# A decode step of two attention and two MLP layers: each 8 MB cache load split into even and odd partitions on two DMA queues

## The chip, the cores and the metric

The kernel runs on one core of one Trainium2 chip. The core's engines are TensorE (PE, with its weight loads as PEld), VectorE (DVE), ScalarE (ACT), GpSimd (POOL) and SyncE (SP, which here only issues DMAs); 16 DMA engines move the data between the chip's main memory (HBM) and the on-chip memory. The metric is the device time of one execution in microseconds (us), as the median of several runs; lower is better.

## What is computed

Two layers of attention over a cache, each followed by a gated MLP, for a batch of 2 and one new token each. Cut to what matters here:

```python
B, Sq, D = 2, 1, 576
H, Sk, Dh = 32, 8192, 128            # k_cache and v_cache: (B, H, Sk, Dh) float32, 268 MB each

def attention(x):
    q = (x @ wq) split into H heads of Dh
    scores = einsum("bhqd,bhkd->bhqk", q, k_cache) * Dh ** -0.5
    o = einsum("bhqk,bhkd->bhqd", softmax(scores), v_cache)
    return o joined @ wo

def mlp(x):
    return (gelu(x @ w_gate) * (x @ w_up)) @ w_down      # 576 -> 4608 -> 576

x = x + attention(layernorm(x));  x = x + mlp(layernorm(x))
x = x + attention(layernorm(x));  x = x + mlp(layernorm(x))
```

Both attention layers read the whole of both caches, so nearly every byte is read twice.

## The kernel before, in words

One work item of attention is a pair of heads of one batch entry (30 pairs), or one head alone (the last two heads, 4 items; the kernel calls them singles). Layer 0 takes the 30 pairs and then the singles, layer 1 the same in reverse order, so that some cache data of the singles can stay on the chip between the layers.

**Memory.** One tile, `space`, holds everything that is loaded: 128 partitions by 24 parts and a little more; a part is 2048 float32 per partition. For the pairs it is three slots of 8 parts, at parts 0, 8 and 16 (`slots0` and `slots1`, lines 255 and 256). The keys of a pair fill one slot and its values another, so that K and V of pair after pair go round the three slots. A slot's load is 128 partitions by 16384 float32, 8192 KB; partition p gets one contiguous piece of 64 KB.

**Order of the loads.** All loads stand in one queue in the program, `sp.queue`, in a fixed order. `pump` (line 97) issues the load at its head as soon as the program has reached the point at which its place is free; `done` (line 157) frees a place and pumps. For the pairs that makes two points for each item n: when the last products of K(n) have been summed (`add_up`, line 652), its slot takes V(n+1), and when `values(n)` (line 731) has used V(n), its slot takes K(n+2). Each load is one DMA on SyncE's queue (line 171). The tile framework, not the kernel, adds the semaphore waits: each instruction waits for those whose data it reads or overwrites, as far as the framework can tell their regions of `space` apart.

**The work of one item.** `multiply(n, unit)` (line 617) takes the keys in five units of 2, 2, 2, 1 and 1 parts. VectorE multiplies the keys by the query in place (line 637: input and output are the same region of `space`), GpSimd adds the two halves of each row in place (line 642), VectorE sums the rest to scores (line 656). Then come the maximum (line 691 and 698 on VectorE, with TensorE between and after), the exponentials on ScalarE (line 705 and 709), and `values(n)`: 64 matrix products on TensorE that read the slot of V(n) (line 739). What they made is gathered later, during item n+1 (lines 755 to 774). VectorE runs its instructions in order, so the first multiplication of item n+1 stands right behind the maximum of item n.

In the first 6 items of layer 1 and the last 4 of layer 0 a quarter of the rows of a unit is summed by ScalarE (line 646) in place of GpSimd. Weights (`rows`, `middle`, `out_rows`, `down` and so on) are loaded by DMAs of their own on SyncE's queue, at line 185 and the like. In layer 1 the first pair's K and V come in halves of 4 parts each. So 8-part loads are K and V of 30 pairs in layer 0 without the first K, which comes in two halves, and of 29 pairs in layer 1: 59 and 58, 117 in all.

The functions that the diff touches, and what calls them:

Of the kernel before, what the change touches and what calls it, by code (L numbers as in the profile page):

```python
# [24 lines left out]
PART = 16 * DH  # L25
# [106 lines left out]
def decode_layers(ctx, tc, x_in, kc, vc, wq, wo, wg, wu, wd, out):  # L132
    nc = tc.nc
# [8 lines left out]
    space = consts.tile([P, END], F32, name="space")  # L142
# [19 lines left out]
    def cache(kind, layer, item, at, lo=0, hi=None, skip=0):  # L162

        hi = item.parts if hi is None else hi
        src = {"k": kc, "v": vc}[kind][item.b, item.h:item.h + item.heads].rearrange("h s d -> (h s) d")
        src = src.rearrange("(p j) d -> p (j d)", p=P)
        base = (kind, layer) + item.name

        def load(a):
            at_of[base] = a - skip - lo * PART  # L170
            nc.sync.dma_start(space[:, a:a + (hi - lo) * PART - skip], src[:, lo * PART + skip:hi * PART])

        sp.queue.append(([base + (k,) for k in range(lo, hi)], at + lo * PART + skip, (hi - lo) * PART - skip, load))

# [842 lines left out]
```

## Time and profile before

| | before |
|---|---|
| median of 3 runs | 2685.91 us (2685.9 to 2685.99) |
| the profiled execution, its own time | 2685.71 us |
| its span, first to last instruction | 2683.9 us |
| VectorE busy | 1863.1 us (69%) |
| GpSimd busy | 1143.9 us (43%) |
| TensorE busy | 935.0 us (35%) |
| ScalarE busy | 180.5 us (7%) |
| read from HBM | 1151.6 MB |

The span is what the trace covers; 1.8 us of the execution's own time lie outside it. Busy times are sums over an engine's instructions. A row of the timeline has the start in us from the span's start, the duration, the engine, the line, the operation and its tiles; in brackets stands the idle time before it on its engine and what ended it. "SPq" and "ACTq" are the sequencers of SyncE and ScalarE issuing a DMA; that row's start is when the issue's waits were over.

### The profile page before, as it was taken

To read this page: it belongs to the slowest core of one execution; us is meant where nothing else is said; L and a number is where in the kernel's file an instruction comes from. 1 tells how busy PE (TensorE), PEld (TensorE's weight loads), DVE (VectorE), ACT (ScalarE), POOL (GpSimd) and SP (SyncE) were. 2 spreads that over 40 slices of the span, in tenths; PEclk is the share of its full clock that TensorE was granted. 3 is DMA by queue.
4 is the path that set the end of the run, shared out by engine and by line. 5 is a ranking of instruction groups with operands and counts; after the bars stand their busy time and mean duration, and the time that the engine had idled before them with its cause. 6 is when DMAs were issued, how large, how long until landed. Compare 5 with 4: busy or idle time off the path is not lost.

```text
span 2683.9 us, 18550 instructions
## 1 busy us (share of the span) xinstructions
PE 935.0 (35%) x7356; PEld 328.4 (12%) x7356; DVE 1863.1 (69%) x1349; ACT 180.5 (7%) x918; POOL 1143.9 (43%) x342
## 2 busy tenths in 40 slices
PE   2322332233233323326665233233323332332255
PEld 0010111011001101102221011001100110110022
DVE  5578777867777787787158777787677778777750
ACT  0000000000000000003013100000000000000000
POOL 2345444544544454454024444454454445444530
PEclk7656665665666566657986666566656656665667
DMA  9999999999999999999999999999999999999998
GB/s 422 435 437 426 432 436 436 432 429 434 434 433 432 433 433 434 434 427 420 408 410 436 435 433 433 433 430 432 437 434 431 430 435 436 434 426 436 435 422 375
DMA packets 37911, 1152.81 MB, mean 430 GB/s; under 512 B 4272, under 2 KB 4928, under 8 KB 16448
## 3 DMA queue, kind: packets, MB, share of 16 engines
q1 hardware_dynamic: 37800, 1151.62, 99.8%
q8 instruction: 58, 0.95, 0.1%
q14 instruction: 29, 0.24, 0.0%
q10 hardware_dynamic: 24, 0.01, 0.0%
HBM read 1151.60 MB, written 0.00 MB: 429 GB/s over the span
## 4 chain that ended last, share of the span: by engine, by line
DMA 27%; DVE 13%; PE 7%; POOL 6%; issue 1%; ACT 1%; POOLq 0%; SPq 0%; ACTq 0%; DVEq 0%
DMA space<-in_A_k_cache_dram 19%; DVE space L637 8%; POOL space L642 6%; PE acc L739 6%; DVE S L656 4%; DMA space<-in_B_w_down_dram 3%; DMA space<-in_B_w_gate_dram 1%; DMA space<-in_A_v_cache_dram 1%; DMA space<-in_B_w_up_dram 1%; DMA space<-in_A_wq_dram 1%; DVE osb L757 1%; ACT prz L709 1%; DMA space<-in_A_wo_dram 1%; PE xps L784 0%; PE sm L700 0%
## 5 line engine op out<-in xcount | busy, mean ns | idle before, releaser
L642 POOL TENSOR_TENSOR space<-space 128x2048 f32<-128x2048 f32 (+3 forms) x332 | 1140.4, 3443 | 1315.5 <-DVE space L637 1211.1
L637 DVE TENSOR_TENSOR space<-space,qp 128x4096 f32<-128x4096 f32 (+2 forms) x329 | 1126.9, 3441 | 460.9 <-DMA space<-in_A_k_cache_dram 450.5
L656 DVE TENSOR_REDUCE S<-space 128x32 f32<-128x2048 f32 (+3 forms) x332 | 581.9, 1753 | 114.9 <-POOL space L642 112.0
L739 PE MATMUL acc<-space,prz 128*8 128x512 f32 x4096 | 594.4, 743 | 8.1 <-issue 6.7
L768 PE MATMUL spare<-weights,osb 128*64 128x2 f32 (+1 forms) x528 | 70.8, 256 | 1199.6 <-ACT osb L759 1183.1
L768 PEld LDWEIGHTS spare<-weights,osb 128*64 128x64 f32 (+1 forms) x528 | 65.2, 208 | 1216.2 <-ACT osb L759 1198.1
L739 PEld LDWEIGHTS acc<-space,prz 128*8 128x8 f32 x4096 | 112.8, 103 | 423.3 <-issue 418.7
L693 PE MATMUL sm<-ident,m 128*1 128x128 f32 x68 | 24.9, 366 | 330.1 <-DVE m L691 330.1
L759 ACT COPY osb<-osb 128x128 f32<-128x128 f32 x60 | 17.9, 298 | 1731.5 <-DVE osb L757 1731.5
L757 DVE SCALAR_TENSOR_TENSOR osb<-acc,diag,osb 128x128 f32<-128x128 f32 x204 | 71.5, 351 | 7.2
L462 POOL TENSOR_TENSOR rstd<-ve,mhalf 128x2 f32<-128x2 f32 x4 | 2.8, 700 | 162.7 <-DVE ve L461 162.7
L719 PE MATMUL sm<-rs,one 128*128 128x2 f32 x120 | 34.9, 360 | 81.1 <-ACT prz L709 81.1
L646 ACT ACTIVATE space<-space 128x128 f32<-128x128 f32 x188 | 55.6, 297 | 66.5 <-DVE space L637 51.1
L709 ACT ACTIVATE prz<-S,nbs 64x128 f32<-64x128 f32 (+1 forms) x136 | 53.4, 393 | 3.1
L693 PEld LDWEIGHTS sm<-ident,m 128*1 128x1 f32 x68 | 5.4, 79 | 342.1 <-DVE m L691 309.4
L700 PE MATMUL sm<-m,one 1*128 1x2 f32 (+1 forms) x136 | 38.7, 351 | 22.8 <-DVE m L698 22.7
L698 DVE TENSOR_REDUCE m<-sm 1x2 f32<-1x128 f32 (+1 forms) x68 | 18.9, 278 | 32.5 <-PE sm L693 32.5
L719 PEld LDWEIGHTS sm<-rs,one 128*128 128x128 f32 x120 | 29.7, 307 | 86.3 <-ACT prz L709 86.3
L755 DVE TENSOR_SCALAR osb<-acc,diag 128x128 f32<-128x128 f32 x68 | 23.3, 342 | 23.7 <-PE acc L739 23.7
L903 DVE STREAM_TRANSPOSE turned<-acc 128x288 f32<-128x288 f32 x4 | 1.9, 483 | 52.2 <-PE acc L892 52.2
L705 ACT ACTIVATE nbs<-sm 128x2 f32<-128x2 f32 (+1 forms) x68 | 11.7, 172 | 390.7 <-PE sm L700 390.7
L700 PEld LDWEIGHTS sm<-m,one 1*128 1x128 f32 x136 | 32.8, 298 | 41.3 <-DVE m L698 41.1
(130 smaller groups left out, 452.3 us busy)
## 6 DMA issues: line engine op xcount, KB each, us to landing
space<-in_A_k_cache_dram SPq DMA_DIRECT2D x8, 4096.0 KB, 19.1
space<-in_A_v_cache_dram SPq DMA_DIRECT2D x3, 4096.0 KB, 21.1
space<-in_A_v_cache_dram SPq DMA_DIRECT2D x6, 2048.0 KB, 32.8
space<-in_B_w_gate_dram SPq DMA_DIRECT2D x18, 576.0 KB, 8.2
space<-in_B_w_up_dram SPq DMA_DIRECT2D x18, 576.0 KB, 7.8
space<-in_A_wo_dram SPq DMA_DIRECT2D x16, 576.0 KB, 8.7
space<-in_A_wo_dram SPq DMA_DIRECT2D x8, 1152.0 KB, 27.3
space<-in_B_w_gate_dram SPq DMA_DIRECT2D x2, 4608.0 KB, 19.6
```

Of the source, the lines that this page charges most:

```text
L637: nc.vector.tensor_tensor(out=u, in0=t, in1=qp_of(n)[:, 0:DH].unsqueeze(1).to_broadcast([P, r1 - r0, DH]), op=ALU.mult)
L642: nc.gpsimd.tensor_tensor(out=half, in0=half, in1=u[:, :r2 - r0, DH // 2:], op=ALU.add)
L646: nc.scalar.activation(row, row, AF.Copy, accum_out=S[n][:, 16 * lo + r:16 * lo + r + 1])
L656: nc.vector.tensor_reduce(out=S[n][:, r0:r1], in_=half, axis=AX.X, op=ALU.add)
L693: nc.tensor.transpose(peaks[n], m, ident)
L700: nc.tensor.matmul(low[n], one[0:1, :].to_broadcast([1, P]), m1, start=True, stop=True)
L709: nc.scalar.activation(prz[rows_, 0:item.rows // 4, e, :], s[rows_, 0:item.rows].rearrange("p (g r) -> p g r", r=4), AF.Exp, bias=nbs[rows ...
L719: nc.tensor.matmul(tot, ones, rs[:, n % 2, :], start=True, stop=True)
L739: nc.tensor.matmul(acc_of(n)[32 * c:32 * c + 8, :], prz[:, g, :, :].rearrange("p e r -> p (e r)"), space[:, at:at + 4 * DH], start=(g < 4) ...
L755: nc.vector.tensor_scalar_mul(t, q[:, 0, :], diag[:, 0:1])
L757: nc.vector.scalar_tensor_tensor(t, q[:, r, :], diag[:, r:r + 1], t, op0=ALU.mult, op1=ALU.add)
L768: nc.tensor.matmul(to[:, i, 0:item.heads], t[:, i:item.heads * DH:GH], w, start=True, stop=True,)
```

## The change

A load of eight parts becomes two DMAs. The even partitions (`space[0::2, ...]`, 64 partitions by 16384) go to SyncE's queue and the odd ones (`space[1::2, ...]`) to ScalarE's. Loads of fewer parts stay one DMA on SyncE's queue. Five lines are added, so the lines below 171 count 5 more in the changed kernel: 637 becomes 642, 691 becomes 696, and so on.

```diff
         def load(a):
             at_of[base] = a - skip - lo * PART
-            nc.sync.dma_start(space[:, a:a + (hi - lo) * PART - skip], src[:, lo * PART + skip:hi * PART])
+            queues = (nc.sync, nc.scalar) if hi - lo == 8 else (nc.sync,)
+            step = len(queues)
+            for r, queue in enumerate(queues):
+                queue.dma_start(
+                    space[r::step, a:a + (hi - lo) * PART - skip], src[r::step, lo * PART + skip:hi * PART]
+                )
```

The instructions of the built programs, engine by engine, show where the new DMAs stand and what waits for them. Names in brackets are semaphores that an instruction waits for. DVE, PE, Activation and Pool count an engine's finished instructions; DMAHW0 to DMAHW7 count landed DMAs, and the DMAs take the eight in turn.

**SyncE**, from the load of V(1) on, before: one DMA for each load, alternately V (after a DVE count) and K (after a PE count).

```order
L171 DMA space<-in_A_v_cache_dram 128x16384 [waits DMAHW4_49,DMAHW1_49,DVE_49]
L171 DMA space<-in_A_k_cache_dram 128x16384 [waits DMAHW2_49,PE_49]
L171 DMA space<-in_A_v_cache_dram 128x16384 [waits DMAHW3_49,DVE_49]
L171 DMA space<-in_A_k_cache_dram 128x16384 [waits DMAHW4_49,PE_49]
L171 DMA space<-in_A_v_cache_dram 128x16384 [waits DMAHW5_49,DVE_49]
```

The same place of SyncE now: the same sequence of loads with 64 partitions each.

```order
L174 DMA space<-in_A_v_cache_dram 64x16384 [waits DMAHW1_49,DVE_49]
L174 DMA space<-in_A_k_cache_dram 64x16384 [waits DMAHW3_49,PE_49]
L174 DMA space<-in_A_v_cache_dram 64x16384 [waits DMAHW5_49,DVE_49]
L174 DMA space<-in_A_k_cache_dram 64x16384 [waits DMAHW7_49,PE_49]
L174 DMA space<-in_A_v_cache_dram 64x16384 [waits DMAHW1_49,DVE_49]
```

The other 64 partitions are with **ScalarE**. Its instructions of item 0 and the start of item 1's, before (nbs and prz are the softmax, osb and oT the gathering):

```order
L705 ACTIVATE nbs<-sm_125 128x2 [waits PE_49]
L709 ACTIVATE prz,rs<-S,nbs 64x32x4 [waits Activation_49]
L709 ACTIVATE prz,rs<-S,nbs 64x32x4
L759 COPY osb<-osb 128x128 [waits DVE_49]
L774 COPY oT<-spare 32x4 [waits PE_49]
L774 COPY oT<-spare 32x4
L705 ACTIVATE nbs<-sm_126 128x2 [waits PE_49,Activation_49]
```

And now, from the load of V(1) on:

```order
L174 DMA space<-in_A_v_cache_dram 64x16384 [waits DMAHW1_49,DVE_49]
L710 ACTIVATE nbs<-sm_125 128x2 [waits PE_49]
L714 ACTIVATE prz,rs<-S,nbs 64x32x4 [waits Activation_49]
L714 ACTIVATE prz,rs<-S,nbs 64x32x4
L174 DMA space<-in_A_k_cache_dram 64x16384 [waits DMAHW2_49,PE_49]
L764 COPY osb<-osb 128x128 [waits DVE_49]
L779 COPY oT<-spare 32x4 [waits PE_49]
L779 COPY oT<-spare 32x4
L174 DMA space<-in_A_v_cache_dram 64x16384 [waits DMAHW4_49,DVE_49]
L710 ACTIVATE nbs<-sm_126 128x2 [waits PE_49,Activation_49]
```

Two DMA issues, each with its wait, have come into every item of ScalarE: the V load stands ahead of the softmax, the K load between the softmax and the gathering.

**VectorE** before, from the end of item 1 to the start of item 2: the first multiplication waits for one DMA, which is K(2).

```order
L691 TENSOR_REDUCE m<-S 128x1 [waits DVE_49]
L698 TENSOR_REDUCE m_302<-sm_126 1x2 [waits PE_49]
L637 TENSOR_TENSOR space<-space,qp_123 128x4096 [waits DMAHW5_49]
L637 TENSOR_TENSOR space<-space,qp_123 128x4096
L656 TENSOR_REDUCE S<-space 128x32 [waits Activation_49,Pool_49]
```

The same place now:

```order
L696 TENSOR_REDUCE m<-S 128x1 [waits DVE_49]
L703 TENSOR_REDUCE m_307<-sm_126 1x2 [waits PE_49]
L642 TENSOR_TENSOR space<-space,qp_123 128x4096 [waits DMAHW4_49,DMAHW5_49,DMAHW3_49,DMAHW2_49]
L642 TENSOR_TENSOR space<-space,qp_123 128x4096
L661 TENSOR_REDUCE S<-space 128x32 [waits Activation_49,Pool_49]
```

The counts that belong to these four waits name the two halves of V(2) (on 2 and 3) and the two halves of K(3) (on 4 and 5). The halves of K(2), on 0 and 1, are no longer waited for here: item 1's first multiplication has waited for them, together with those of V(1) on 6 and 7. So it goes on through the pairs of both layers: the first multiplication of item n waits for V(n) and K(n+1), which are loaded into the other two slots. The matrix products of `values(n)` wait for the two halves of V(n) alone, as they waited for the one DMA before.

## The prediction

> **What bounds the kernel now.** I read the page's slices first: is any resource busy from end to end?
>
> ```profile
> PE 935.0 (35%) x7356; PEld 328.4 (12%) x7356; DVE 1863.1 (69%) x1349; ACT 180.5 (7%) x918; POOL 1143.9 (43%) x342
> DMA  9999999999999999999999999999999999999998
> q1 hardware_dynamic: 37800, 1151.62, 99.8%
> ```
>
> The DMA engines are, in all 40 slices, and everything comes from one queue, q1, SyncE's. Next, the rate by stretches (the last two columns are DMA share and GB/s): the pairs of layer 0, and the first MLP with its small pieces.
>
> ```profile
> 60.00:560.00 500.00, 156.48 (x1045) 51.63 (x1045) 359.51 (x224) 22.25 (x101) 226.89 (x63) 0.61 1.00 433
> 1262.00:1402.00 140.00, 91.42 (x1262) 38.27 (x1258) 40.12 (x91) 11.47 (x66) 12.37 (x9) 0.90 1.02 406
> ```
>
> A load of 8192 KB (8.389 MB) at 433 GB/s takes 19.37 us, and K and V of a pair 38.75. The timeline of one item shows how the engines stand to that.
>
> ```profile
> 502.16 0.33 SPq L171 DMA_DIRECT2D space<-in_A_v_cache_dram  x1
> 503.93 0.17 ACT L705 ACTIVATE nbs<-sm 128x2 f32<-128x2 f32 x1 [5.90 <-PE sm L700]
> 510.62 8.75 DVE L637 TENSOR_TENSOR space<-space,qp 128x4096 f32<-128x4096 f32 x2 [7.43 <-DMA space<-in_A_k_cache_dram]
> 514.34 0.33 SPq L171 DMA_DIRECT2D space<-in_A_k_cache_dram  x1
> 540.86 0.33 SPq L171 DMA_DIRECT2D space<-in_A_v_cache_dram  x1
> 544.39 9.70 PE L739 MATMUL acc<-space,prz 128*8 128x512 f32 x64
> 549.33 8.75 DVE L637 TENSOR_TENSOR space<-space,qp 128x4096 f32<-128x4096 f32 x2 [7.44 <-DMA space<-in_A_k_cache_dram]
> 554.16 0.33 SPq L171 DMA_DIRECT2D space<-in_A_k_cache_dram  x1
> ```
>
> Item n's multiplication starts at 510.62, when K(n) has landed, and the next at 549.33: 38.71 us, the DMA time of two loads. The compute of K(n) takes until 540.86, 30.24 us, when its slot is given to V(n+1); K(n+2) follows at 554.16, when the matrix products have used V(n). So VectorE waits 7.4 us for each K, and the DMAs never stop, **because two loads are still queued or running while K(n) is being worked on**. That is what the change touches.
>
> **The change part by part.** *The added waits.* The rows of VectorE in the section on the change show that the first multiplication of item n now waits for V(n) and K(n+1). Put this on the timeline above: the multiplication that starts at 510.62 would have to wait for a K load that is issued only at 514.34. The wait cannot be met early; it binds in every item. While it lasts all three slots are full (K(n), V(n), K(n+1)), so no load can be issued until K(n) is worked off. The multiplication and the loads, which overlapped, go one after the other:
>
> - at 0 the multiplication starts, and the DMAs are idle;
> - at 30.24 K(n)'s slot is free and V(n+1) is issued into an empty queue;
> - at about 43.5 (554.16 less 510.62) `values(n)` is done and K(n+2) is issued, behind the running V(n+1), without a gap;
> - V(n+1) and K(n+2) land, and item n+1 starts.
>
> What a load into an empty queue costs beside its bytes is shown by the first load of the program. It has 4096 KB, and SyncE's fourth DMA (line 207) waits for it to land:
>
> ```profile
> 0.73 0.39 SPq L171 DMA_DIRECT2D space<-in_A_k_cache_dram  x1
> 12.87 0.54 SPq L207 DMA_DIRECT2D space<-in_A_wq_dram  x1
> SPq L207 <- DMA space<-in_A_k_cache_dram: 9.6, 1, 9.6
> ```
>
> 4.194 MB at 433 GB/s are 9.69 us; from issue to the waiter's start it is 12.14, so start and landing cost 2.45. The period is 30.24 + 2.45 + 38.75 = **71.44 us** in place of 38.71. The last pair of a layer waits for its V alone: 30.24 + 2.45 + 19.37 = 52.06.
>
> How many periods there are, from the multiplications' starts: second and last pair of layer 0, first, second and last pair of layer 1.
>
> ```profile
> 84.61 8.75 DVE L637 TENSOR_TENSOR space<-space,qp 128x4096 f32<-128x4096 f32 x2 [17.86 <-DMA space<-in_A_k_cache_dram]
> 1171.45 8.75 DVE L637 TENSOR_TENSOR space<-space,qp 128x4096 f32<-128x4096 f32 x2 [7.53 <-DMA space<-in_A_k_cache_dram]
> 1439.41 4.40 DVE L637 TENSOR_TENSOR space<-space,qp 128x4096 f32<-128x4096 f32 x1
> 1475.39 8.75 DVE L637 TENSOR_TENSOR space<-space,qp 128x4096 f32<-128x4096 f32 x2 [6.37 <-DMA space<-in_A_k_cache_dram]
> 2562.91 8.75 DVE L637 TENSOR_TENSOR space<-space,qp 128x4096 f32<-128x4096 f32 x2 [7.48 <-DMA space<-in_A_k_cache_dram]
> ```
>
> Layer 0: pair 0, which started long before 84.61, now waits for V(0) and K(1), and K(1)'s landing is what 84.61 waited for. So pair 0 starts at 84.61, and the last one 28 periods and one short one later: 84.61 + 28 x 71.44 + 52.06 = 2137.0, against 1171.45: **+965.5**. Layer 1: pair 0 now waits for K(1), whose landing 1475.39 waited for; the last pair starts 2052.4 later, against 2562.91 - 1475.39 = 1087.5: **+964.9**. Three items near the layers' starts have a compute of 27 to 28.5 us in place of 30.24, which these rows bound (pair 0 of layer 1 is worked off when V(1) is issued):
>
> ```profile
> 37.13 8.75 DVE L637 TENSOR_TENSOR space<-space,qp 128x4096 f32<-128x4096 f32 x2 [9.89 <-PE qp L595]
> 65.62 0.33 SPq L171 DMA_DIRECT2D space<-in_A_v_cache_dram  x1
> 1467.96 0.33 SPq L171 DMA_DIRECT2D space<-in_A_v_cache_dram  x1
> 1502.54 0.33 SPq L171 DMA_DIRECT2D space<-in_A_v_cache_dram  x1
> ```
>
> That is 28.49, 28.55 and 27.15, together 6.5 less than three times 30.24. Behind each layer's last pair the work goes on as before, except that V of that pair has landed where it was just being loaded; this lead is worth between nothing and one load, 19.37 us, per layer. The next loads wait for slots that the last pair's compute frees at an unchanged distance, which speaks for nothing; I take 0 and keep 39 for the range.
>
> Sum: 965.5 + 964.9 - 6.5 = 1923.9 us on the profiled execution's 2685.7 (its span of 2683.9 and 1.8 outside; the median is 0.2 more): **4610 us**.
>
> *The second issue, on ScalarE.* 117 issues; the longest that I found of this line takes 0.59 us.
>
> ```profile
> 13.45 0.59 SPq L171 DMA_DIRECT2D space<-in_A_k_cache_dram  x1
> ACT osb L759 <- DVE osb L757: 1731.5, 60, 40.1
> ```
>
> The V issue stands ahead of nbs, but is released at 502.16 by the same maximum that nbs needs, by way of TensorE and VectorE, until 503.93: 1.77 us cover 0.59. The K issue waits for TensorE's products, ahead of the gathering copy, which waits for those products itself (1731.5 us in all). I cost both at nothing; without cover it is 0.59 for each of 59 V loads, 35 us. Nothing is queued on ScalarE that somebody else waits for in the meantime.
>
> *Two queues in place of one.* The trace has no two bulk queues at once, so I bound the rate: not above 437 GB/s, the best slice, and not below 406, the MLP stretch with its small pieces.
>
> ```profile
> GB/s 422 435 437 426 432 436 436 432 429 434 434 433 432 433 433 434 434 427 420 408 410 436 435 433 433 433 430 432 437 434 431 430 435 436 434 426 436 435 422 375
> ```
>
> At 437 a load takes 19.20 us, at 406 20.66: -0.17 to +1.29 for each of the 114 loads that are now on the path, -19 to +147 us. The bytes per partition stay 64 KB, so I take 433. The 2.45 us at an empty queue were paid once at the program's start; at least the issue of 0.33 remains, so the sum may be 58 x 2.12 = 123 us lower.
>
> **The rivals.** *The waits cost nothing.* Place: the head of each pair on VectorE. If the loads waited for had landed when VectorE gets there, the time would be set by the queues alone: the same 16 engines move the same bytes, 2685.7 us; or, if two queues run at 437, 117 x 0.17 = 20 less, 2666. It decides if K(n+1) is issued more than 21.8 us (2.45 + 19.37) ahead of item n's start; the timeline has it 3.7 us behind. Only if the rows' counts mean other loads than I read can this be. [...]
>
> *Only V(n) binds.* If the wait for K(n+1) were no obstacle, a period would be 52.06: 2685.7 + 58 x 13.35 = 3460 us. For it speaks only that V is the earlier of the two; the four semaphores in the row speak against it.
>
> *The halves are slow.* 64 stepped partitions might use half of the DMA engines' paths. If each load took twice as long, a period would be 30.24 + 2.45 + 77.5 = 110.2, and the time 2685.7 + 58 x 71.5 = 6830 us. Against it: the MLP's `middles` load 64 stepped partitions within the 406 GB/s stretch.
>
> **How the numbers follow.** The forecast has a chance of 0.86, no cost 0.04, V alone 0.03, slow halves 0.03, and 0.04 for what I do not see. Within the forecast the bounds are 4610 - 123 - 19 = 4468 and 4610 + 147 + 35 = 4792; the ends would need all of one side together, so I take **4480 to 4760**. What this measurement tells from no change is about 0.2% (5.4 us): faster 0.02, within 0.02, slower 0.96.
>
> **What would show it.** Right: in the slices DMA falls from 9 to 5 (38.75 of 71.4), GB/s to about 235 in the pairs; VectorE's idle time ahead of its multiplication grows from 7.4 to some 40 us per item, ended by a DMA; multiplications start about 71.4 apart; the V issue still comes 30.2 after the start. Wrong: a distance of 38.7 (no cost) or 52 (V alone), or a distance beyond 73 with packets that run below 433 GB/s while they run. If the compute no longer takes 30.24, or the empty queue costs other than 2.45, the mechanism stands and the size is off.

## The result, and the profile after

The changed kernel takes 4682.92 us (median of 5 runs, 4680.89 to 4683.82) against 2685.91: 1.743 times the time before, with a 95% interval of 1.741 to 1.745. The forecast was 4610, with a range of 4480 to 4760. The sign and the mechanism held; the sum was 73 us short.

The page of the changed kernel first: the engines' busy times, the DMA share in 40 slices, what the DMAs moved in them, the two queues, and the group of VectorE's multiplications (line 642 now) with the idle time before them and what ended it.

```profile
PE 928.6 (20%) x7356; PEld 327.9 (7%) x7356; DVE 1862.9 (40%) x1349; ACT 180.5 (4%) x918; POOL 1144.3 (24%) x342
DMA  7655646546465464656994645546455464564648
GB/s 314 269 215 216 270 179 269 224 207 278 180 260 224 206 286 172 259 225 255 418 416 211 287 188 242 251 180 287 188 242 251 188 279 206 224 260 179 278 207 363
...
q1 hardware_dynamic: 30312, 660.88, 33.8%
q10 hardware_dynamic: 9384, 490.75, 24.3%
...
L642 DVE TENSOR_TENSOR space<-space,qp 128x4096 f32<-128x4096 f32 (+2 forms) x329 | 1126.8, 3440 | 2468.8 <-DMA space<-in_A_k_cache_dram 2424.5
```

No engine has more to do than before: VectorE's 1862.9 us and GpSimd's 1144.3 are the old sums. What fell is the DMA row, from 9 in every slice to 4 to 6 in the slices of the pairs; only the two around the first MLP, where the loads are not split, still show 9 (the first and the last slice, which hold other work too, show 7 and 8). VectorE's idle time before its multiplications has grown from 460.9 to 2468.8 us, by 2007.9, and the kernel by 1997.0. The windows of the two layer-0 stretches (the last two columns are DMA share and GB/s) put a number on it: 0.54 of the engines' time, where the forecast had 38.75 of 71.44, and 229 to 231 GB/s, where it had about 235.

```profile
100.00:900.00 800.00, 131.21 (x883) 43.53 (x883) 314.59 (x193) 18.74 (x85) 200.60 (x56) 0.56 0.54 231
900.00:2000.00 1100.00, 183.59 (x1215) 61.12 (x1215) 435.05 (x275) 26.39 (x120) 277.66 (x77) 0.56 0.54 229
```

One period on the timeline, from the release of a V slot to the next (SPq and ACTq are the two issuing sequencers):

```profile
986.57 0.47 SPq L174 DMA_DIRECT2D space<-in_A_v_cache_dram  x1
986.57 0.50 ACTq L174 DMA_DIRECT2D space<-in_A_v_cache_dram  x1
988.34 0.17 ACT L710 ACTIVATE nbs<-sm 128x2 f32<-128x2 f32 x1 [5.89 <-PE sm L705]
990.10 9.04 PE L744 MATMUL acc<-space,prz 128*8 128x512 f32 x64
999.21 0.47 SPq L174 DMA_DIRECT2D space<-in_A_k_cache_dram  x1
999.21 0.50 ACTq L174 DMA_DIRECT2D space<-in_A_k_cache_dram  x1
1029.82 8.75 DVE L642 TENSOR_TENSOR space<-space,qp 128x4096 f32<-128x4096 f32 x2 [42.22 <-DMA space<-in_A_k_cache_dram]
1060.03 0.47 SPq L174 DMA_DIRECT2D space<-in_A_v_cache_dram  x1
```

This is the sequence that was forecast: V(n+1) is issued when K(n) is worked off, 30.21 us after its multiplication began (1060.03 less 1029.82); K(n+2) follows 12.64 us later behind the running V(n+1); and the next multiplication starts only when both have landed, here 43.25 us after the V issue. ScalarE's issue falls on the same moment as SyncE's, and nbs still starts 1.77 us after it, as before.

### The profile page after: what moved, and what is told of

It reads as the page before. It is cut to its first block, busy times and chain, and to the rows that moved or that the text cites. A ratio compares the mean times of both kernels' runs of the same rounds, so it can differ in the third digit from the quotient of the medians.

```text
span 4679.1 us, 18957 instructions
## 1 busy us (share of the span) xinstructions
PE 928.6 (20%) x7356; PEld 327.9 (7%) x7356; DVE 1862.9 (40%) x1349; ACT 180.5 (4%) x918; POOL 1144.3 (24%) x342
## 5 line engine op out<-in xcount | busy, mean ns | idle before, releaser
L642 DVE TENSOR_TENSOR space<-space,qp 128x4096 f32<-128x4096 f32 (+2 forms) x329 | 1126.8, 3440 | 2468.8 <-DMA space<-in_A_k_cache_dram 2424.5
L705 PE MATMUL sm<-m,one 1*128 1x2 f32 (+1 forms) x136 | 38.8, 352 | 22.7 <-DVE m L703 22.6
L651 ACT ACTIVATION_READ_ACCUMULATOR space<-space 128x1 f32 x188 | 35.1, 187 | 0.0
L937 PE MATMUL xps<-space,hT 128*2 128x144 f32 x576 | 26.4, 328 | 17.7 <-DMA space<-in_B_w_down_dram 16.3
```

The costliest lines, as they stand in the source:

```text
L642: nc.vector.tensor_tensor(out=u, in0=t, in1=qp_of(n)[:, 0:DH].unsqueeze(1).to_broadcast([P, r1 - r0, DH]), op=ALU.mult)
L651: nc.scalar.activation(row, row, AF.Copy, accum_out=S[n][:, 16 * lo + r:16 * lo + r + 1])
L705: nc.tensor.matmul(low[n], one[0:1, :].to_broadcast([1, P]), m1, start=True, stop=True)
L937: nc.tensor.matmul(xps[32 * c:32 * c + B, 0:CW], hT[t // 2][:, t % 2 * NI + i, :], space[:, a:a + CW], start=piece == downs[layer][0] and ...
```

## The experiments

The theory: the four added waits make the multiplications and the loads take turns, and nothing else of the change matters. The rivals: the second queue, ScalarE's part in it, or the shape of the halves. All times are medians, ratios stand against the kernel before. Diffs are against the changed kernel.

**One queue for both halves.** The waits stay, the second queue and ScalarE's issues go.

```diff
-            queues = (nc.sync, nc.scalar) if hi - lo == 8 else (nc.sync,)
+            queues = (nc.sync, nc.sync) if hi - lo == 8 else (nc.sync,)
```

> Both stepped halves of every 8-part load go to SyncE's queue; ScalarE issues none. The instructions wait for the same loads as in the changed kernel. Theory (the added waits on VectorE serialize compute and loads): unchanged against the changed kernel, 4683 us within 1% (4640 to 4730). Rival (the second queue, or issuing from ScalarE, slows the stream): 2686 us within 1%.

Measured: 4672.89 us, ratio 1.740 (1.737 to 1.743). The loss is there without the second queue. The second queue and ScalarE's issues account together for the last 10 us, 0.2 per period.

**Stepped halves on two queues, without the waits.** Each load goes as two column pieces of four parts, each split into even and odd partitions on the two queues. In this form the built program has no added wait.

```diff
-            for r, queue in enumerate(queues):
-                queue.dma_start(
-                    space[r::step, a:a + (hi - lo) * PART - skip], src[r::step, lo * PART + skip:hi * PART]
-                )
+            n = (hi - lo) * PART - skip
+            for c in range(step):
+                p, q = c * n // step, (c + 1) * n // step
+                for r, queue in enumerate(queues):
+                    queue.dma_start(
+                        space[r::step, a + p:a + q], src[r::step, lo * PART + skip + p:lo * PART + skip + q]
+                    )
```

> Every 8-part load still goes even partitions to SyncE's and odd ones to ScalarE's queue, but in two pieces of 4 parts each, so four DMAs of 64 partitions by 8192. In the built program the first multiplication then waits only for its own K. Theory: all bytes still go stepped by two queues, yet the time is back at 2686 us, within 0.5% (2672 to 2700). Rival (stepped halves on two queues are slow to transfer): 4000 us or more.

Measured: 2695.41 us, ratio 1.0035 (1.0023 to 1.0047). Stepped halves on two queues run at 431 GB/s, so the transport is not the loss:

```profile
100.00:900.00 800.00, 249.25 (x1649) 84.02 (x1653) 587.84 (x375) 36.91 (x168) 373.26 (x103) 0.61 1.00 431
```

**The minimal pair.** One queue; a load is a whole piece and two stepped halves of the remaining columns. Only the width of the stepped part differs: 12800 columns, as in the diff, or 13312. The lines stand in place of the changed kernel's `queues`, `step` and loop.

```diff
+            n = (hi - lo) * PART - skip
+            edge = 12800 if hi - lo == 8 else 0
+            nc.sync.dma_start(space[:, a:a + n - edge], src[:, lo * PART + skip:hi * PART - edge])
+            if edge:
+                for r in range(2):
+                    nc.sync.dma_start(space[r::2, a + n - edge:a + n], src[r::2, hi * PART - edge:hi * PART])
```

The bytes, the number of DMAs, their order and the partitions are alike. The first multiplication of item 0, in the built programs with 12800 and with 13312 columns:

```order
L642 TENSOR_TENSOR space<-space,qp_123 128x4096 [waits DMAHW0_49,PE_49]
L642 TENSOR_TENSOR space<-space,qp_123 128x4096 [waits DMAHW4_49,DMAHW6_49,DMAHW3_49,DMAHW7_49,DMAHW0_49,PE_49]
```

Four semaphores more, those of the stepped halves of V(0) and K(1): at this width the framework no longer keeps a stepped region apart from other slots that the multiplication doesn't touch. GpSimd's additions, which run behind the multiplication, get the same four waits. Why the step lies between these two widths no run here shows.

> All on SyncE's queue. Each 8-part load is three DMAs: the first 3584 columns over all 128 partitions, the last 12800 columns as even and odd partitions. In the built program the first multiplication waits for its own K alone. Theory: 2686 us within 1%. Rival (stepped halves are slow to transfer): 78% of the bytes stepped, above 4000 us.

> As the run with 12800 columns, but 3072 columns whole and 13312 stepped: the transfers are 4% different, and in the built program the first multiplication now waits for V of its item and K of the next. Theory: nearly the whole loss is back; the first 3072 columns of V are issued while K is still worked on and take 3.6 us off a period of 73, so about 4480 us (4380 to 4700). Rival (the transfers, not the waits, set the time): within 2% of the run with 12800.

Measured: 2694.73 us (ratio 1.0033, 1.0019 to 1.0047) and 4468.23 (1.6635, 1.6587 to 1.6684). Two successive multiplications of each, the narrower first:

```profile
942.21 8.75 DVE L642 TENSOR_TENSOR space<-space,qp 128x4096 f32<-128x4096 f32 x2 [7.65 <-DMA space<-in_A_k_cache_dram]
981.00 8.75 DVE L642 TENSOR_TENSOR space<-space,qp 128x4096 f32<-128x4096 f32 x2 [7.53 <-DMA space<-in_A_k_cache_dram]
```

```profile
912.15 8.75 DVE L642 TENSOR_TENSOR space<-space,qp 128x4096 f32<-128x4096 f32 x2 [38.46 <-DMA space<-in_A_k_cache_dram]
981.73 8.75 DVE L642 TENSOR_TENSOR space<-space,qp 128x4096 f32<-128x4096 f32 x2 [38.33 <-DMA space<-in_A_k_cache_dram]
```

They are 38.79 us apart in the first and 69.58 in the second. 512 columns more in the stepped part cost 1773 us, and beside those columns the added waits are what the two programs differ in. Together with the run before it, in which every 8-part load goes stepped and next to nothing is lost, this shows the cause.

**Which wait binds.** Only the V loads split, or only the K loads.

```diff
-            queues = (nc.sync, nc.scalar) if hi - lo == 8 else (nc.sync,)
+            queues = (nc.sync, nc.scalar) if hi - lo == 8 and kind == "v" else (nc.sync,)
```

> Only V loads of eight parts are split into even and odd partitions on the two queues; K loads stay whole on SyncE's queue. In the built program the first multiplication of an item waits for its own K and for its V. Theory: a period is the compute of K, 30.4 us, and one V load into an empty queue, 22 to 23 us (the last pairs of the changed kernel stand 52.9 and 53.7 us apart): 2686 + 58 x 14.5 = 3530 us (3470 to 3590). Rival (each split load costs its share, half of the loads half of the loss): 3685 us.

> Only K loads of eight parts are split; V loads stay whole on SyncE's queue. The first multiplication of an item waits for the next item's K, whose load stands behind V's. Theory: waiting for the later of the two loads is the whole loss, so the time is that of the changed kernel, 4680 us (4620 to 4730), though half of the loads are as before. Rival (each split load costs its share): 3685 us.

Measured: V alone 3539.89 us (ratio 1.318, 1.314 to 1.322), K alone (the same line with "k") 4625.19 (1.722, 1.717 to 1.727). A row of each, V first:

```profile
971.82 8.75 DVE L642 TENSOR_TENSOR space<-space,qp 128x4096 f32<-128x4096 f32 x2 [21.48 <-DMA space<-in_A_v_cache_dram]
```

```profile
1023.24 8.75 DVE L642 TENSOR_TENSOR space<-space,qp 128x4096 f32<-128x4096 f32 x2 [41.39 <-DMA space<-in_A_k_cache_dram]
```

The wait for K(n+1) alone makes nearly the whole loss, 1939 of 1997 us; the wait for V(n) would make 854 by itself. They don't add up, because K(n+1) is issued 12.6 us after V(n) and in the changed kernel stands behind it on both queues (in the period at 986.57 V lands 23.4 and 23.6 us after its issue, and K's last half 43.2 us after that issue): who waits for the second has waited for the first.

**Other ways of halving.** Halves by columns (128 partitions by 8192) on two queues and on one, and halves by blocks (partitions 0 to 63 and 64 to 127) on two queues and on one. None of the four has an added wait. The forms on one queue have `(nc.sync, nc.sync)` as in the first run. The column form with two queues, where `size` is half of the columns:

```diff
-                queue.dma_start(
-                    space[r::step, a:a + (hi - lo) * PART - skip], src[r::step, lo * PART + skip:hi * PART]
-                )
+                lo_, hi_ = r * size, r * size + size
+                queue.dma_start(space[:, a + lo_:a + hi_], src[:, lo * PART + skip + lo_:lo * PART + skip + hi_])
```

> The halves are columns: 128 partitions by 8192 float32 on SyncE's queue and the other 8192 columns on ScalarE's; no added waits. Theory: 2686 us within 0.5%. Rival (two queues gain): 2666 us.

> Each 8-part load as two DMAs of 128 partitions by 8192 columns, both on SyncE's queue: the same pieces as in the run with column halves on two queues (2695.3), with one queue. Theory A (the second queue costs the 9 us: engines turn from one queue to the other): 2686 to 2687. Theory B (more and smaller DMAs cost them, about 0.08 us for each DMA added, wherever it is queued): 2694 to 2696.

Measured: 2695.27 us on two queues (ratio 1.0035, 1.0022 to 1.0048), 2694.85 on one (1.0033, 1.0021 to 1.0046). The second queue costs nothing here. The 9 us aren't a matter of the number of DMAs either, as the second theory of the expectation for one queue had it, though its time came true: two, three and four DMAs to a load (the three are those of the 12800 columns) all give 2694.7 to 2695.4. What these four kernels share is that each partition's 64 KB go in two packets. The packet rows of before, and of the forms with two and with four DMAs to a load:

```profile
DMA packets 37911, 1152.81 MB, mean 430 GB/s; under 512 B 4272, under 2 KB 4928, under 8 KB 16448
```

```profile
DMA packets 54761, 1152.84 MB, mean 428 GB/s; under 512 B 6144, under 2 KB 6800, under 8 KB 18320
```

```profile
DMA packets 58510, 1152.89 MB, mean 428 GB/s; under 512 B 9888, under 2 KB 10544, under 8 KB 22064
```

Without the packets under 512 B these are 33639, 48617 and 48622, some 14980 more in both, or 936 for each of 16 engines. 9 us over 936 packets are 10 ns each. That is argued from four times that agree, not tried by itself.

The block form:

```diff
-            step = len(queues)
+            size = P // len(queues)
             for r, queue in enumerate(queues):
+                p = slice(r * size, r * size + size)
                 queue.dma_start(
-                    space[r::step, a:a + (hi - lo) * PART - skip], src[r::step, lo * PART + skip:hi * PART]
+                    space[p, a:a + (hi - lo) * PART - skip], src[p, lo * PART + skip:hi * PART]
                 )
```

> The halves are partitions 0 to 63 (SyncE) and 64 to 127 (ScalarE) in place of even and odd; no added waits in the built program. Theory: 2686 us within 0.5%, if each queue's half is spread over all 16 DMA engines. [...]

> Each 8-part load as two DMAs, partitions 0 to 63 and then 64 to 127, both on SyncE's queue, so that the halves stand one behind the other. It tells why halves of neighbouring partitions moved at half the rate on two queues. Theory A (64 neighbouring partitions reach only half of something that the 16 engines write through, whatever the queue): a DMA of the lower half runs at half rate, then one of the upper half, and the time is 4800 to 5300 with packets near 4800 ns. Theory B (the two queues of neighbouring blocks collide): full rate, 2686 to 2700, packets near 2420 ns.

Measured: 4844.3 us on two queues (ratio 1.797, 1.789 to 1.805) and 5129.46 on one (1.910, 1.906 to 1.913). The runs on two queues spread from 4779.0 to 4873.6, so their ratio is known less well than the others. The theory for them, no loss, missed. On one queue the first theory came true. Both forms take about as long as the changed kernel, by another cause, which the slices show (two queues first, then one):

```profile
DMA  9999999999999999999999999999999999999997
GB/s 277 215 213 215 216 222 235 221 223 220 222 225 227 224 225 224 233 232 244 406 412 227 223 223 230 231 229 231 230 239 234 239 216 216 215 218 218 225 230 315
```

```profile
DMA  9999999999999999999999999999999999999998
GB/s 278 209 208 205 210 210 211 211 210 207 210 208 210 212 211 211 210 208 237 392 413 209 208 209 209 212 210 209 211 211 207 211 208 210 212 207 211 207 210 339
```

The DMA engines are busy throughout and move half as much (from 100 to 900 us a share of 1.00 at 220 and 209 GB/s; before had 433 there). In the changed kernel they are idle nearly half of the time and move at the full rate in between (231 GB/s at a share of 0.54 make 428). Read by GB/s alone, the two can't be told apart; the DMA row beside it does. With one queue the slices of the pairs have 205 to 212 GB/s, so 64 neighbouring partitions alone are served at half rate, and 64 stepped ones are not: in the run with 12800 columns, on one queue too, 78% of a load go stepped and the engines move 431. What makes the blocks slow no run shows. Nor is it settled why two queues with a block each, which together write all 128 partitions, get no more than 213 to 239. Worked out from these rates and 16 busy engines, 64 KB take an engine 4.4 to 4.9 us there; a packet of that size took 2.42 before.

**Whole loads by turns.** K on SyncE's queue and V on ScalarE's, nothing split.

```diff
-            queues = (nc.sync, nc.scalar) if hi - lo == 8 else (nc.sync,)
-            step = len(queues)
-            for r, queue in enumerate(queues):
-                queue.dma_start(
-                    space[r::step, a:a + (hi - lo) * PART - skip], src[r::step, lo * PART + skip:hi * PART]
-                )
+            queue = nc.scalar if hi - lo == 8 and kind == "v" else nc.sync
+            queue.dma_start(space[:, a:a + (hi - lo) * PART - skip], src[:, lo * PART + skip:hi * PART])
```

> Whole 8-part loads, K on SyncE's queue and V on ScalarE's, by turns: two queues without any split. Theory A (a second queue costs time by itself): 2690 to 2696. Theory B (only the number and size of the DMAs cost): 2685 to 2687, as before. A gain, under 2684, would need a rate above 433 GB/s with two queues.

Measured: 2762.63 us, ratio 1.0283 (1.0269 to 1.0297). Both theories miss it. The multiplications alternate:

```profile
927.81 8.75 DVE L638 TENSOR_TENSOR space<-space,qp 128x4096 f32<-128x4096 f32 x2 [0.21 <-DMA space<-in_A_k_cache_dram]
976.47 8.75 DVE L638 TENSOR_TENSOR space<-space,qp 128x4096 f32<-128x4096 f32 x2 [17.36 <-DMA space<-in_A_k_cache_dram]
1008.06 8.75 DVE L638 TENSOR_TENSOR space<-space,qp 128x4096 f32<-128x4096 f32 x2 [0.32 <-DMA space<-in_A_k_cache_dram]
```

48.66 us, then 31.59: two items take 80.25 where they took 77.42, and 29 such pairs of items would make 82 us, where 77 were lost. With one queue the loads land in the order of their issue (before, from 480 to 700 us, V lands 27.9 us after its issue, and K, issued 13.3 us later, 35.0 us after its own); with two, a K and a V that are under way together share the engines, so that one item has its K early and the next has it late. In the short half nobody waits for a load and VectorE is the bound (28.71 of 31.59 us busy). The DMA engines lose a little in both halves (share and GB/s in the last two columns; before had 1.00 and 433 in the pairs):

```profile
927.81:976.47 48.66, 23.84 (x153) 7.04 (x153) 28.70 (x18) 2.91 (x13) 18.28 (x5) 0.64 0.97 417
976.47:1008.06 31.59, 1.75 (x11) 1.37 (x11) 28.71 (x18) 0.61 (x3) 18.20 (x5) 0.50 0.99 421
```

The alternation and the lower rate are measured; that the sharing makes them is argued.

**Why the periods were longer than forecast.** 128 more TensorE instructions per pair, behind its last products, so that more instructions have to be fetched while the loads run.

```diff
+            if item.heads == 2:
+                spin(qp[1], 64)
```

Here `spin` is the kernel's own helper; it makes 64 products of no use, each with its weight load, into a spare corner of the query tile `qp`.

> The changed kernel with 128 more matrix products and weight loads on TensorE behind the last products of every pair, which nobody waits for; the output stays the reference's. It tests why the landing of V(n+1) and K(n+2) took longer than forecast. Theory: packets of instruction fetch (16384 bytes, on one DMA engine at a time) push that engine's share of the load back, and the multiplication waits for the last engine; more TensorE instructions mean more such packets while loads run, about twice as many, so that nearly every period is a slow one (about 73.4 us in place of a mix of 71.9 and 73.4), and the time rises by 58 times some 0.5 us, to 4700 to 4720. Rival: the packets have nothing to do with it, the slow periods come from the weight of the loads or their addresses, and the time stays at 4683 within 5 us.

Measured: 4743.79 us, ratio 1.766 (1.763 to 1.769), 24 to 44 us more than expected. In the changed kernel the 56 full waits of VectorE for a K fall into two groups with nothing between: 21 of 40.56 to 41.02 us (mean 40.78) and 35 of 41.77 to 42.77 (mean 42.16). A period of each, by the issue of V and the multiplication, and the queues in between (packets, MB, share of the 16 engines):

```profile
258.51 0.47 SPq L174 DMA_DIRECT2D space<-in_A_v_cache_dram  x1
300.33 8.75 DVE L642 TENSOR_TENSOR space<-space,qp 128x4096 f32<-128x4096 f32 x2 [40.79 <-DMA space<-in_A_k_cache_dram]
```

```profile
q1 hardware_dynamic: 160, 8.39, 48.3%
q10 hardware_dynamic: 160, 8.39, 46.6%
```

```profile
q1 hardware_dynamic: 160, 8.39, 46.5%
q10 hardware_dynamic: 160, 8.39, 44.9%
q8 instruction: 1, 0.02, 0.1%
```

The first takes 41.82 us; the second, the period shown at 986.57, takes 43.25 and has one packet of instruction fetch (queue q8, 16 KB) in it. So it is throughout the trace: each of the 35 long waits has one such packet while its loads run, and none of the 21 short ones has (three of these have a smaller one, 8 KB of queue q14, and stay short). With 118 such packets in place of 58, all 56 waits have one or two and lie between 41.80 and 43.05 (mean 42.17): the short group is gone. The waits of VectorE over the whole kernel, the changed one first and then the one with more instructions:

```profile
DVE space L642 <- DMA space<-in_A_k_cache_dram: 2424.5, 58, 55.7
...
DVE space L642 <- DMA space<-in_A_v_cache_dram: 44.0, 2, 22.5
```

```profile
DVE space L642 <- DMA space<-in_A_k_cache_dram: 2453.6, 58, 56.3
...
DVE space L642 <- PE qp L429: 50.9, 2, 26.0
```

The waits for K grow by 29.1 us, as the theory had it (58 times 0.5). The rest is a cost of the experiment that was not foreseen: each layer's last multiplication now waits for the added products (6.9 us more over the two), and from there to layer 1's first pair and to the end it takes 12.1 and 15.6 us more.

## Why the prediction was right, and where its size was off

**The waits, right.** That the first multiplication of item n can't start before K(n+1), that this binds in every item, and that loads and compute take turns: shown by the minimal pair, by V alone (3540, where the rival "only V(n) binds" had worked out 3460) and by the timeline.

**30.24 us of compute, right.** 30.21 in the period shown. **The rate while the loads run, right.** All but the first 16 packets of a period take 2.42 us each, as before, and the split loads without waits ran at 431 GB/s.

**ScalarE's issues at nothing, right.** nbs still follows the issue by 1.77 us, and with one queue, and none of these issues, the time falls by only 10 us.

**2.45 us for an empty queue, the term that was mis-sized.** It was read from one load at the program's start. From issue to multiplication the short group has 41.82, less 38.75 for the bytes: 3.07. The long group has 43.20, or 4.45. Over both layers the starts of the first, second-last and last pair give the mean:

```profile
83.31 8.75 DVE L642 TENSOR_TENSOR space<-space,qp 128x4096 f32<-128x4096 f32 x2 [55.73 <-DMA space<-in_A_k_cache_dram]
...
2123.82 8.75 DVE L642 TENSOR_TENSOR space<-space,qp 128x4096 f32<-128x4096 f32 x2 [40.90 <-DMA space<-in_A_k_cache_dram]
2177.58 8.75 DVE L642 TENSOR_TENSOR space<-space,qp 128x4096 f32<-128x4096 f32 x2 [22.49 <-DMA space<-in_A_v_cache_dram]
2477.44 4.42 DVE L642 TENSOR_TENSOR space<-space,qp 128x4096 f32<-128x4096 f32 x1 [36.70 <-DMA space<-in_A_k_cache_dram]
...
4513.32 8.75 DVE L642 TENSOR_TENSOR space<-space,qp 128x4096 f32<-128x4096 f32 x2 [42.33 <-DMA space<-in_A_k_cache_dram]
4566.08 8.75 DVE L642 TENSOR_TENSOR space<-space,qp 128x4096 f32<-128x4096 f32 x2 [21.50 <-DMA space<-in_A_v_cache_dram]
```

28 periods of 72.88 in layer 0 and 28 of 72.71 in layer 1, against 71.44: 40.3 and 35.6 us. The two short periods are 53.76 and 52.76 against 52.06, 2.4 more. Pair 0 starts 1.3 earlier than forecast, and the 6.5 us taken off for three shorter computes are within the measured mean. Behind the last pairs the way is 12.1 us shorter than before (299.86 from there to layer 1's first pair in place of 303.94, 113.0 to the end in place of 121.0), which the forecast had bounded by 0 and 39 and taken as 0. That this made the miss smaller is luck. Together 40.3 + 35.6 + 2.4 - 1.3 + 6.5 - 12.1 = 71.4; the profiled run is 71.3 over the sum.

Of the 1.4 us per period that were missing, instruction fetch makes 0.86 (35 of 56 periods, each 42.16 less 40.78). The trace has a fetch packet of 16 KB in every long period and in no short one, and the experiment shows that more of them make all periods long. In the long periods the last 64 KB packet ends 0.9 to 2.0 us after all others, in the short ones at most 0.35 us. That the fetch holds back one engine, and that the late packet is this engine's, fits; the trace doesn't name a packet's engine, so it is argued.

The rest is there without any fetch: 0.62 in a short period, 3.07 in place of 2.45. The trace has both cases packet by packet. In the short periods it is 1.26 us on the mean from the issue to the first packet, then 1.15 more than 38.75 to the end of the last, then 0.66 to the multiplication. For the program's first load it is 1.02, 1.02 and 0.41. That the first packets after an idle stretch are slow, 3.1 us each for the first 16 in place of 2.42, is thus no more than a small part of the difference: the first load had it too (1.63 in place of 1.21 for its smaller packets), inside its 2.45. Why the start and the end take longer in the loop stays open.

**The rivals.** "The waits cost nothing", wrong for this change: the waits make the loss. That the halves by themselves change nothing holds within 0.35% for stepped halves without the waits (2695.41 us). It doesn't hold for blocks, which halve the rate (220 and 209 GB/s against 433), though the DMA engines are as busy. "Only V(n) binds" is the run with V alone, not the change. "The halves are slow" was wrong for these halves; the half rate that it assumed is what the blocks have.

## What to carry to other kernels

Before a DMA is split, read the waits of the built program: a region that the framework can't tell apart from its neighbours turns a prefetch into a chain, and here 512 columns decided between 0.3% and 66%. A split that serves no purpose of its own isn't free even without that: two pieces per partition cost 0.3%, whole loads by turns on two queues cost 2.8%, and 64 neighbouring partitions halve the rate (205 to 239 GB/s against 433). When a load restarts on idle engines in every step, measure the restart in the loop (here 3.07 us or 4.45) and not once at the start (2.45).

## What was unexpected of the hardware

- Halves of 64 neighbouring partitions were moved at 205 to 239 GB/s with busy engines; 64 stepped partitions, at 431.
- Waits for loads that have a 16 KB packet of instruction fetch among them are 1.4 us longer (42.16 in place of 40.78, 35 of 35 against 0 of 21).
- Loads that restart after an idle stretch spend 39.7 us of packet time on bytes that take 38.8 in an unbroken stream; their first 16 packets take 3.1 us each in place of 2.42.
